# Units 0 and 1 by seven block products in all four block pairs, early narrowing moved, and the last product split over two tiles

## The chip, the core and the metric

The kernel runs on one core of a Trainium2 chip. Such a core has a matrix engine (PE; its weight loads are listed apart as PEld), a vector engine (DVE), a scalar engine (ACT), GpSimd (POOL) and SyncE (SP); here POOL and SP mostly issue DMAs. The engines run their own instruction lists in order and wait for one another through semaphores. The metric is the device time of one execution in microseconds, as the median of several.

## What is computed

An attention block over 32 memory slots gives x (4608 tokens of 512), a soft mixture of experts turns it into x = c @ slot_out with 32 slots, and a two-layer softplus network follows, cut here to what the change touches:

```python
slot_out = ...                         # 32 x 512, from 8 experts (w1, w2)
x = c @ slot_out                       # 4608 x 512, c is a softmax over 32 slots
h = x @ w_in                           # w_in 512 x 2048
g = np.maximum(h, 0.0) + np.log1p(np.exp(-np.abs(h)))
return g @ w_out                       # w_out 2048 x 512
```

## The kernel before

**Stages.** Attention, the softmaxes and the expert layers take the first 178 us. The sum over all experts stands in two PSUM tiles S; when the last product into S is done, S is copied out and multiplied, and the softplus network begins. Its first layer is shortened: x @ w_in = c @ (slot_out @ w_in), so PE forms G = slot_out @ w_in once (`Gs`) and then h for 128 features and 512 tokens with one product of 512 columns (tile `hp`). CT holds c, transposed in nine groups (`stack`, tiles c4 and ctp, L1177 to L1188).

**Units, blocks, jobs.** The 2048 features are eight units of 256, the 4608 tokens nine blocks of 512. ACT takes softplus of h (PSUM to SBUF), and g is then split in a rounded copy (ACT) and the rest (DVE), since one product in PE's format is not exact enough; each product with w_out is three matrix products (rounded x rounded, rounded x rest, rest x rounded). A job is a block, or a pair of blocks, with some units; `JOBS` lists them in order, and PE works through them in this order (`all_out`).

A plain job (`plain_out`, L1587) needs 24 products of 512 columns for each unit and block. A pair job (`seven_out`, L1720) takes two blocks and the two halves of a unit's 256 features and of the 512 outputs as a 2 x 2 block product, by seven block products in place of eight: 42 products for a unit and two blocks instead of 48. For that DVE forms differences of the two blocks' g (`differences`, four instructions of 1024 elements for two units) and of the weights, and seven splits are needed (`split`: ACT L1666, DVE L1668) where a plain job needs four. The block products, named 1 to 7, stand in two PSUM tiles OB (`ob`); each must be read before its tile is used again. `evacuate` reads them: the first step of an output is a copy (ACT or DVE, L801), a second is an addition on DVE (L1368). An output that was written before is added to in HBM by an accumulating DMA from POOL (L1375); a first write goes by SP (L1379).

Before, the jobs are: blocks 0 to 8 plain with units 0 and 1; block 8 plain with 2 and 3, then the four pairs with 2 and 3; block 8 plain with 4 to 7, then the four pairs with 4 to 7 (two groups of two units, products of 24 instead of 12 instructions). So units 2 to 7 are done by seven products, units 0 and 1 are not.

**Narrowing.** w_in and w_out come as 64-bit floats in sixteen pieces wi0, wo0 to wi7, wo7 (w_in and w_out of a unit). `narrow` (L1090 to L1163) makes a piece 32 bits wide with six DVE instructions (L1107, L1111, L1115, L1120, L1127, L1133). For wo it makes the rounded copy (ACT, L1143) and the rest (DVE, L1145), tile W; and for a unit that is used in pair jobs also four quarter-sized sums and differences (L1158), again split in two (ACT L1161, DVE L1163), tile WS.

**What sets the order.** All is written by a planner (`Flow`): it takes of the steps that could begin first the one of lowest rank, and the numbers in `PLAN` shift the ranks. Buffers are pools: four g buffers (`ng`), two h tiles, four output buffers (`ob`), a few x buffers for softplus results, ten weight slots. Weight pieces are loaded by SP in the order `ko`; `ea` says after which expert the first four are put in.

**The end.** The last product (4 of the last job) goes into the two halves t of one OB tile; `finish(..., apart=True)` adds each half on DVE (L1395) and stores it on its own.

Of the kernel before, what the change touches and what calls it, by code (L numbers as in the profile page):

```python
# [26 lines left out]
    "win": 0.1,  # L27
# [28 lines left out]
    "half": 4,  # L56

    "gs": -3667.66,

    "hs": 658.45,  # L60
# [3 lines left out]
    "ea": (1, 5, 5, 5),  # L64
# [3 lines left out]
    "fh": 710.35,  # L68

    "fG": -11197.15,  # L70

    "fo": 12974.77,

    "fe": -3681.57,

    "nb": 2795.97,

    "ns": 2697.86,

    "pace": PACE,  # L80
# [3 lines left out]
    "ob": 4,  # L84

# [18 lines left out]
    "fx": 11238.0,  # L104
# [9 lines left out]
    "ne": 60,  # L114

    "ha": -3.0,

    "va": 3.0,
# [18 lines left out]
class Flow:  # L137
# [9 lines left out]
    def __init__(self):  # L147
        self.engine = defaultdict(float, D=2.1, V=2.2, G=5.7, A=2.0)
        self.token, self.pools, self.got, self.live = {}, {}, {}, []
        self.now = (0.0, "")  # L150
        self.product, self.moved = None, []
# [76 lines left out]
    def run(self, until):  # L228
        stuck = None
        while any(until(c) for c in self.live):  # L230
# [22 lines left out]
            for i, (e, d) in enumerate(ops):  # L253
                t = max(self.seen(now, e), self.engine[e]) + d
# [12 lines left out]
def tile_slot_attention_soft_moe_softplus_mlp(  # L267
# [775 lines left out]

    def load_wo(u):
        yield [("D", 2.52)], [f"+w8<{NW8}"], 0
# [5 lines left out]
        done(f"wo{u}")  # L1051

    def load_wi(u):
        yield [("D", 2.52)], [f"+w8<{NW8}"], 0
# [5 lines left out]
        done(f"wi{u}")  # L1060
# [33 lines left out]
    def narrow(key, after=(), by_act=False, low_by_act=False):  # L1094
# [49 lines left out]
        yield [("V", 1.2)], []  # L1144
        nc.vector.tensor_tensor(out=w[:, 1], in0=af, in1=w.bitcast(F32)[:, 0], op=ALU.subtract)  # L1145
# [7 lines left out]
        for o, x, y, op in (  # L1153
# [3 lines left out]
            yield [("V", 0.37)], []  # L1157
# [4 lines left out]
        yield [("V", 1.23)], []  # L1162
        nc.vector.tensor_tensor(out=w[:, 1], in0=af, in1=w.bitcast(F32)[:, 0], op=ALU.subtract)  # L1163
# [7 lines left out]
    def stack():  # L1171

        for k in range(NTB):
# [14 lines left out]
            nc.scalar.activation(CT[:, 4 * k : 4 * k + 4], ctp, AF.Copy)  # L1188

# [91 lines left out]

    for n, x in enumerate(EARLY + LATE):
        unit = PLAN["pace"][n]
        after = (unit,) if unit else ()
        flow.add(narrow(x, after, n in PLAN["abs"], n in PLAN["rnd"]), PLAN["nb"] + PLAN["ns"] * n, "fb")
    flow.AFTER = {**flow.AFTER, "D": PLAN["land"]}
    flow.run(lambda c: c[2] == "ex")
# [11 lines left out]
    def narrow_G(nb):  # L1299
# [20 lines left out]
        for u in range(2):  # L1320
            for j in (2 * u, 2 * u + 1):
                yield [("D", 0.45)] * 4, []
# [32 lines left out]
    def evacuate(steps, places):  # L1355
# [16 lines left out]
        for half, tb, before, mine in places:  # L1372
            if before:
                yield [("G", 1.0)], before
                nc.gpsimd.dma_start(out=place(half, tb), in_=o, accum_op=ALU.add)  # L1375
                landed(mine, 6.5)
            else:
                yield [("D", 0.8)], []
                nc.sync.dma_start(out=place(half, tb), in_=o)  # L1379
                landed(mine, 4.0)  # L1380
        flow.later("ob", i, 6.5 if before else 4.0)

    def finish(half, tb, before, begin, steps, apart=False):


        yield [("D", 0.8)], [*before, begin, "+ob"], 0
# [3 lines left out]
        landed(f"fin{half}{tb}", 5.0)  # L1390
        for name, at, release in steps:
            for t in range(1 + apart):
                x = slice(t, t + 1) if apart else slice(0, 2)
                yield [("V", 0.69 if apart else 1.22)], [f"{name}{t if apart else 1}", f"fin{half}{tb}"]
# [5 lines left out]
            done(f"rd{name}")  # L1400
        if not apart:
# [17 lines left out]
    JOBS = PLAN["jobs"]  # L1419
# [147 lines left out]
    def plain_out(j, n, tb, units):  # L1567

        for u in units:
            first_u, last_u = u == units[0], u == units[-1]  # L1570
            for (chunks, t0, t1), now, oc in [
# [7 lines left out]
                yield [("P", 0.233 * len(chunks) * len(now))], (  # L1579
# [23 lines left out]
    def raw(j, side, units, m, chain):  # L1603
# [3 lines left out]
        key = j, side, units  # L1607
        yield [("P", 0.467)], [f"G{u}.0", f"G{u}.1", "+h"] + chain[:1]
# [25 lines left out]
    def differences(j, k, units):  # L1634
# [6 lines left out]
        t2 = X[j][:, k, :n]  # L1641
# [3 lines left out]
        yield [("V", d)], [f"t{j}"]  # L1645
        tt(out=t2, in0=b[:, :, 1], in1=a[:, :, 1], op=ALU.subtract)
# [6 lines left out]
        done(f"d{j}{u}4")  # L1653

    def split(j, q, k, units, chain):
# [15 lines left out]
        if q in ("43" if len(groups(JOBS[j][1])) == 1 else "47"):  # L1671
            free("x", Xi[j, side, units])
        if q == "6" and units[-1] == JOBS[j][1][-1]:
            free("x", Xi[j])
# [9 lines left out]
    def groups(units):  # L1684
        return [units[i : i + 2] for i in range(0, len(units), 2)]

    def runs(units):

        n = len(groups(units))
        if n == 1:  # L1690
            return [(q, 0) for q in "1265734"]
        return [("2", 0), ("1", 0), ("2", 1), ("1", 1), ("3", 0), ("3", 1), ("6", 0), ("6", 1)] + [
            ("5", 0), ("7", 0), ("7", 1), ("5", 1), ("4", 0), ("4", 1)
        ]
# [4 lines left out]
    def seven_out(j, units):  # L1699

        for q, k in runs(units):
            grp = groups(units)[k]
# [27 lines left out]
            free("g", i)  # L1730
        over(j, units)
# [162 lines left out]
```

## Time and profile before

| | |
|---|---|
| time, median of three executions | 584.86 us (584.58 to 586.16) |
| the profiled execution's own time | 586.26 us |
| its span, first to last instruction | 584.5 us |
| PE busy | 558.0 us, 95% |
| DVE busy | 403.4 us, 69% |
| ACT busy | 339.0 us, 58% |

The span is cut into 40 slices on the profile's page; a digit gives an engine's busy tenths, and the row PEclk the clock that PE was granted. From 180 us on PE is full; DVE is full only from about 190 to 262 us.

### The profile page before, as it was taken

To read this page: it belongs to the slowest core of one execution; us is meant where nothing else is said; L and a number is where in the kernel's file an instruction comes from. 1 tells how busy PE (TensorE), PEld (TensorE's weight loads), DVE (VectorE), ACT (ScalarE), POOL (GpSimd) and SP (SyncE) were. 2 spreads that over 40 slices of the span, in tenths; PEclk is the share of its full clock that TensorE was granted. 3 is DMA by queue.
4 is the path that set the end of the run, shared out by engine and by line. 5 is a ranking of instruction groups with operands and counts; after the bars stand their busy time and mean duration, and the time that the engine had idled before them with its cause. 6 is when DMAs were issued, how large, how long until landed. Compare 5 with 4: busy or idle time off the path is not lost.

```text
span 584.5 us, 10019 instructions
## 1 busy us (share of the span) xinstructions
PE 558.0 (95%) x4090; PEld 425.5 (73%) x4090; DVE 403.4 (69%) x519; ACT 339.0 (58%) x488; POOL 67.2 (11%) x84
## 2 busy tenths in 40 slices
PE   8798988999879999999999999999999999999997
PEld 4466664545438788878888888888888888888885
DVE  3677855753484999998893877965745945847743
ACT  3667755323324775565866776568567577576530
POOL 1021231300000000000001111210111220211100
PEclk9999998899979999999999999999999999999999
DMA  8999999999999824422215647662255684775952
GB/s 331 424 417 421 417 419 417 418 412 388 418 417 419 344 90 153 151 111 113 86 73 89 107 75 128 108 106 39 46 80 92 101 120 68 115 125 96 178 100 108
DMA packets 23949, 121.56 MB, mean 208 GB/s; under 512 B 3168, under 2 KB 4832, under 8 KB 15712
## 3 DMA queue, kind: packets, MB, share of 16 engines
q1 hardware_dynamic: 17280, 96.81, 41.3%
q0 software_dynamic: 6624, 24.12, 25.9%
q8 instruction: 32, 0.52, 0.4%
q14 instruction: 13, 0.11, 0.1%
HBM read 85.00 MB, written 35.13 MB: 206 GB/s over the span
## 4 chain that ended last, share of the span: by engine, by line
PE 75%; DVE 16%; DMA 3%; ACT 3%; issue 2%; SPq 0%; POOL 0%; DVEq 0%; POOLq 0%; ACTq 0%
PE ob L1720 39%; PE ob L1587 12%; PE hp L1613 4%; DMA kv<-in_kv_dram 3%; PE hid L1203 3%; PE kvp L493 2%; DVE arena L1120 2%; DVE g L1552 2%; PE S L1237 2%; PE idle L920 2%; DVE arena L1133 1%; PE rp L573 1%; PE sc L612 1%; DVE arena L1111 1%; DVE arena L1115 1%
## 5 line engine op out<-in xcount | busy, mean ns | idle before, releaser
L1587 PE MATMUL ob<-g,W 128*128 128x512 f32 x576 | 138.1, 390 | 0.3 <-ACT outs L801 0.3
L1720 PE MATMUL ob<-g,WS 128*128 128x512 f32 x576 | 135.1, 389 | 0.0
L1587 PEld LDWEIGHTS ob<-g,W 128*128 128x128 f32 x576 | 107.7, 188 | 23.8 <-ACT outs L801 1.2
L1720 PEld LDWEIGHTS ob<-g,WS 128*128 128x128 f32 x576 | 108.1, 188 | 22.4
L1720 PE MATMUL ob<-g,W 128*128 128x512 f32 x432 | 100.5, 389 | 0.0
L1668 DVE TENSOR_TENSOR g<-arena,g 128x1024 fp32r<-128x1024 f32 x56 | 67.8, 1222 | 46.6 <-ACT g L1666 46.5
L801 ACT ACTIVATE outs<-ob 128x1024 f32<-128x1024 f32 x61 | 62.5, 1027 | 61.5 <-PE ob L1720 38.6
L1720 PEld LDWEIGHTS ob<-g,W 128*128 128x128 f32 x432 | 81.1, 188 | 16.8
L1375 POOL DMA_DIRECT2D out_dram<-outs x46 | 40.3, 896 | 393.8 <-ACT outs L801 299.5
L1666 ACT ACTIVATE g<-arena 128x1024 fp32r<-128x1024 f32 x56 | 59.2, 1058 | 25.2 <-PE ob L1720 21.1
L1624 ACT ACTIVATE arena<-hp 128x1024 f32<-128x1024 f32 x32 | 32.1, 1021 | 5.7 <-DVE g L1668 3.9
L1552 DVE TENSOR_TENSOR g<-arena,g 128x1024 fp32r<-128x1024 f32 (+1 forms) x26 | 27.3, 1057 | 8.2 <-ACT g L801 6.2
L1668 DVE TENSOR_TENSOR g<-room,g 128x1024 fp32r<-128x1024 f32 x14 | 17.0, 1222 | 20.7 <-ACT g L1666 20.7
L801 ACT ACTIVATE g<-arena 128x1024 fp32r<-128x1024 f32 (+1 forms) x24 | 22.8, 952 | 14.4 <-PE ob L1587 13.6
L1613 PE MATMUL hp<-CT,Gs 128*128 128x512 f32 x96 | 28.9, 389 | 0.0
L920 PE MATMUL idle<-zero 128*128 128x512 bf16 x99 | 27.4, 417 | 1.5 <-POOL zero L923 1.5
L1539 ACT ACTIVATE arena<-hp 128x1024 f32<-128x1024 f32 (+1 forms) x26 | 23.1, 889 | 9.6 <-PE hp L1504 8.8
L666 POOL TENSOR_TENSOR a<-s,ssm 128x512 f32<-128x512 f32 (+1 forms) x20 | 18.8, 961 | 62.9 <-DVE r L465 24.7
L1668 DVE TENSOR_TENSOR g<-x,g 128x1024 fp32r<-128x1024 f32 x14 | 17.0, 1220 | 9.5 <-ACT g L1666 9.5
L1613 PEld LDWEIGHTS hp<-CT,Gs 128*128 128x128 f32 x96 | 18.0, 188 | 3.7
L493 PE MATMUL kvp<-kv,et 128*32 128x128 f32 x512 | 18.6, 275 | 1.7 <-DMA kv<-in_kv_dram 1.7
L920 PEld LDWEIGHTS <-zero 128*128 128x128 bf16 x99 | 9.9, 107 | 13.6 <-issue 5.9
(188 smaller groups left out, 721.5 us busy)
## 6 DMA issues: line engine op xcount, KB each, us to landing
w<-in_moe_w_dram SPq DMA_DIRECT2D x31, 1024.0 KB, 19.9
out_dram<-outs POOLq DMA_DIRECT2D x46, 512.0 KB, 5.4
kv<-in_kv_dram SPq DMA_DIRECT2D x7, 2304.0 KB, 25.0
out_dram<-outs SPq DMA_DIRECT2D x20, 512.0 KB, 2.8
q<-in_q_dram SPq DMA_DIRECT2D x8, 1024.0 KB, 21.7
wi<-in_w_in_dram SPq DMA_DIRECT2D x8, 1024.0 KB, 17.4
wo<-in_w_out_dram SPq DMA_DIRECT2D x8, 1024.0 KB, 17.5
phi<-in_phi_dram SPq DMA_DIRECT2D x8, 576.0 KB, 19.6
```

The source lines that it names most:

```text
L493: nc.tensor.matmul(kvp[32 * h : 32 * h + 32], lhsT=rows[:, 32 * h : 32 * h + 32], rhs=rows_of[:, c, h] if c < SC else rest[:, h], start=(c ...
L801: nc.scalar.activation(o, i, AF.Copy)
L920: nc.tensor.matmul(idle[0], lhsT=zero[:, :128], rhs=zero, start=True, stop=True)
L1375: nc.gpsimd.dma_start(out=place(half, tb), in_=o, accum_op=ALU.add)
L1539: nc.scalar.activation(x, hp, AF.Softplus)
L1552: nc.vector.tensor_tensor(out=g[:, 1, i, t], in0=x, in1=g.bitcast(F32)[:, 0, i, t], op=ALU.subtract)
L1587: nc.tensor.matmul(bank(oc), lhsT=W[u][:, w, i, c], rhs=hb[tb, u][:, x, i], start=(fresh and i == chunks[0] and k == "0"), stop=(stop and ...
L1613: nc.tensor.matmul(hp[:, i], lhsT=Gs[:, 128 * fc : 128 * fc + 128], rhs=CTf[:, TB * tb : TB * tb + TB], start=True, stop=True,)
L1624: nc.scalar.activation(X[key][:, m], hp, AF.Softplus)
L1666: nc.scalar.activation(g[:, 0], x, AF.Copy)
L1668: nc.vector.tensor_tensor(out=g[:, 1], in0=x, in1=g.bitcast(F32)[:, 0], op=ALU.subtract)
L1720: nc.tensor.matmul(OB[at][:, t], lhsT=(W if w == "W" else WS)[u][:, x, c, cols], rhs=g[:, y, m], start=(fresh and u == grp[0] and n == 0), ...
```

## The change

**Jobs.** Units 0 and 1 are now plain in block 8 alone and go through all four pairs as single-group pair jobs. Units 4 and 5, and 6 and 7, get block 8 and three pairs each, and the last pair with all four of these units is the final job. There are 19 jobs: 0 is block 8 with units 0, 1; 1 to 4 are the pairs with them; 5 is block 8 with 2, 3; 6 to 9 the pairs; 10 block 8 with 4, 5; 11 to 13 three pairs; 14 block 8 with 6, 7; 15 to 17 three pairs; 18 the last pair with 4 to 7. In jobs 1, 3, 6 and 9 (`apart`) each block product is read by its own copy and added in HBM; in the others products are still added on DVE.

**Counts from the changed program.** L1587 has 192 products (576 before), L1720 and the new `last_out` 1344 (1008), `hp` 144 as before. DVE has 112 splits L1668 (84), 64 differences (48), 35 whole and three half additions from PSUM (17 and 2), 5 whole and 6 half plain splits L1552 (20 and 8), 32 quarter sums (24). The rest of W and WS is made on DVE ten times (14); for wo3, wo4 and wo7 it is made by ACT (the negative) and an accumulating DMA from POOL (`lower`). POOL issues 66 DMAs (46).

**Order around S.** Of the early pieces, `ea` puts the last three after expert 4 instead of 5, and the ranks now come from a due time for each job less a lead for each kind of step. On DVE, just ahead of the last products into S, this stood before (c are the groups of `stack`, waited for by PE; the L11xx between are the narrowing of wo0 and wi1, in their shared work space arena):

```order
L1179 TENSOR_TENSOR c_2268<-room,c_2268 128x8x32
L1107 TENSOR_SCALAR arena_1948<-wo 128x1024
L1111 TENSOR_SCALAR arena_1948<-arena_1948 128x1024
L1115 TENSOR_SCALAR arena_1948<-arena_1948 128x1024
L1120 SCALAR_TENSOR_TENSOR arena_1948<-wo,arena_1948 128x1024
L1127 TENSOR_SCALAR arena_1948<-wo 128x1024
L1179 TENSOR_TENSOR c_2307<-room,c_2307 128x8x32
```

And now, ahead of the same last two groups:

```order
L1208 TENSOR_TENSOR c_2256<-room,c_2256 128x8x32
L1164 ISA arena_1954<-arena_1954 128x2048 x2
L1208 TENSOR_TENSOR c_2306<-room,c_2306 128x8x32
L1123 TENSOR_TENSOR W<-arena_1954,W 128x1024
L1188 TENSOR_TENSOR arena_1954<-arena_1954 128x256 x2
L1208 TENSOR_TENSOR c_2321<-room,c_2321 128x8x32
L1188 TENSOR_TENSOR arena_1954<-arena_1954 128x256 x2
L1208 TENSOR_TENSOR c_2340<-room,c_2340 128x8x32
```

The narrowing of wo0 and wi1 has moved ahead of groups 5 and 6, and only two and a half instructions stand between the last groups.

**Order of DVE in the first pair job.** In job 1 the splits of units 0 and 1 (L1741), their differences (L1706 to L1716) and the narrowing of later pieces (L1138 to L1164) now share DVE:

```order
L1741 TENSOR_TENSOR g<-room,g 128x1024
L1716 TENSOR_TENSOR room<-room,arena_2521 128x2x512
L1741 TENSOR_TENSOR g<-x_2526,g 128x1024
L1164 ISA arena_2521<-arena_2521,arena_1954 128x2048
L1138 TENSOR_SCALAR arena_2521<-wi 128x1024
L1142 TENSOR_SCALAR arena_2521<-arena_2521 128x1024
L1741 TENSOR_TENSOR g<-x_2526,g 128x1024
```

Before, a plain split L1552 stood between the same narrowing instructions, one for 24 products of PE; now one for 12, and differences with it.

**The end on PE.** The last rows before, block products 5 and 4 (ob_2504 and ob_2503 are the two tiles OB):

```order
L1720 MATMUL ob_2504<-g,WS 128x512 x24
L1720 MATMUL ob_2503<-g,WS 128x512 x12
L1720 MATMUL ob_2504<-g,W 128x512 x24
```

And now:

```order
L1788 MATMUL ob_2524<-g,WS 128x512 x24
L1788 MATMUL ob_2523<-g,WS 128x512 x12
L1816 MATMUL ob_2524<-g,W 128x512 x12
L1816 MATMUL ob_2523<-g,W 128x512 x12
```

Product 4's second half now has the other tile, which product 5 must have left.

```diff
 PLAN = {
-    "ea": (1, 5, 5, 5),
+    "ea": (1, 4, 4, 4),
+    "low": (7, 9, 10, 13, 15),
+    "apart": (1, 3, 6, 9),
     "jobs": (
-        tuple((tb, (0, 1)) for tb in range(9))
-        + ((8, (2, 3)),) + tuple((pair, (2, 3)) for pair in ((0, 1), (2, 3), (4, 5), (6, 7)))
-        + ((8, (4, 5, 6, 7)),) + tuple((pair, (4, 5, 6, 7)) for pair in ((0, 1), (2, 3), (4, 5), (6, 7)))
+        (8, (0, 1)), ((2, 3), (0, 1)), ((6, 7), (0, 1)), ((0, 1), (0, 1)), ((4, 5), (0, 1)),
...
+        (8, (6, 7)), ((4, 5), (6, 7)), ((0, 1), (6, 7)), ((2, 3), (6, 7)), ((6, 7), (4, 5, 6, 7)),
     ),
...
+    def lower(w, af, name, by_dma):
+        if by_dma:
+            yield [("A", 1.06)], []
+            nc.scalar.activation(w[:, 1], af, AF.Copy, scale=-1.0)
+            yield [("G", 1.0), ("D", 3.14)], [], 1
+            nc.gpsimd.dma_start(out=w.bitcast(F32)[:, 1], in_=af, accum_op=ALU.add)
+            landed("l" + name, 2.3)
+            yield [], ["l" + name]
+        else:
+            yield [("V", 1.22)], []
+            nc.vector.tensor_tensor(out=w[:, 1], in0=af, in1=w.bitcast(F32)[:, 0], op=ALU.subtract)
...
         for name, at, release in steps:
-            for t in range(1 + apart):
+            for t, part, b in ((0, 0, at), (1, 0, at), (1, 1, at ^ 1)) if apart else ((0, 1, at),):
                 x = slice(t, t + 1) if apart else slice(0, 2)
-                nc.vector.tensor_tensor(out=o[:, x], in0=OB[at][:, x], in1=o[:, x], op=ALU.add)
-                if apart:
+                nc.vector.tensor_tensor(out=o[:, x], in0=OB[b][:, x], in1=o[:, x], op=ALU.add)
+                if apart and t == part:
...
+    def last_out(j, units):
+        at = bank_of(j, "4")
+        w, c, half = OF["4"]
+        for t in range(2):
+            o = at ^ t
+            for k, grp in enumerate(groups(units)):
...
+                        nc.tensor.matmul(
+                            OB[o][:, t],
+                            lhsT=W[u][:, x, c, cols],
+                            rhs=item[j, "4", grp][0][:, y, m],
+                            start=(t == 1 and k == m == n == 0),
...
-        flow.add(narrow(x, after, n in PLAN["abs"], n in PLAN["rnd"]), PLAN["nb"] + PLAN["ns"] * n, "fb")
+        flow.add(
+            narrow(x, after, n in PLAN["abs"], n in PLAN["low"]),
+            use[u] - LEAD["n" + kind] + PLAN["jit"][n], "fb",
+        )
...
-            flow.add(evacuate(steps, [order(o, where[side])]), PLAN["fe"], "fb")
+            for steps in [[x] for x in steps] if j in PLAN["apart"] else [steps]:
+                flow.add(evacuate(steps, [order(o, where[side])]), due[j, adds[0], 0] + 2.8 - LEAD["e"], "fb")
```

## Rows read from the trace of the kernel before

**Rows 1.** Products of 512 columns: line, count, busy us, mean ns, idle before

```profile
L1587 PE MATMUL ob<-g,W 128*128 128x512 f32 x576 | 138.1, 390 | 0.3 <-ACT outs L801 0.3
L1720 PE MATMUL ob<-g,WS 128*128 128x512 f32 x576 | 135.1, 389 | 0.0
L1720 PE MATMUL ob<-g,W 128*128 128x512 f32 x432 | 100.5, 389 | 0.0
```

**Rows 2.** Busy us by stretch: PE, PEld, DVE, ACT, POOL, clock, DMA share, GB/s

```profile
160.50:164.30 3.80, 0.03 (x1) 0.00 (x0) 3.69 (x6) 1.85 (x3) 0.00 (x0) 1.00 1.00 416
166.00:172.00 6.00, 5.52 (x54) 2.17 (x46) 5.66 (x7) 0.77 (x2) 0.00 (x0) 0.50 1.00 412
...
190.00:262.00 72.00, 71.97 (x371) 58.64 (x369) 70.03 (x90) 45.66 (x55) 0.00 (x0) 1.00 0.47 172
...
310.00:390.00 80.00, 80.00 (x354) 66.25 (x353) 61.28 (x54) 51.80 (x53) 13.02 (x15) 1.00 0.64 102
```

**Rows 3.** The chain that ended last, its last stretch of PE: start, us, what

```profile
516.23 63.93 PE ob L1720 x282
```

**Rows 4.** Around S, by start: PE's last groups and experts, SP's last load

```profile
164.31 0.66 PE L1185 MATMUL ctp<-ident,c 128*128 128x128 f32 x4 [3.77 <-DVE c L1179]
164.89 2.91 PE L1203 MATMUL hid<-w,room 128*32 128x256 f32 x32
...
175.69 2.80 PE L1237 MATMUL S<-w,hT 128*32 128x256 f32 x48
...
181.67 0.50 PE L1504 MATMUL hp<-CT,Gs 128*128 128x512 f32 x1
...
157.22 2.77 SPq L1038 DMA_DIRECT2D w<-in_moe_w_dram  x2
```

**Rows 5.** The same last load (L1038, the two halves of the last w2), issue to landing

```profile
DMA to landing us min/median/max: 17.5/18.1/18.7
```

**Rows 6.** DVE by start: differences, additions and splits, narrowing and quarter sums

```profile
295.97 1.23 DVE L1643 TENSOR_TENSOR room<-x,room 128x1024 f32<-128x1024 f32 x1
297.23 1.23 DVE L1646 TENSOR_TENSOR arena<-x,room 128x1024 f32<-128x1024 f32 x1
298.37 1.22 DVE L1649 TENSOR_TENSOR x<-x 128x1024 f32<-128x1024 f32 x1
...
316.77 1.22 DVE L1368 TENSOR_TENSOR outs<-ob,outs 128x1024 f32<-128x1024 f32 x1
317.90 1.21 DVE L1668 TENSOR_TENSOR g<-x,g 128x1024 fp32r<-128x1024 f32 x1
...
221.18 1.80 DVE L1158 TENSOR_TENSOR arena<-arena 128x256 f32<-128x256 f32 x4
222.90 0.69 DVE L1107 TENSOR_SCALAR arena<-wi 128x1024 int32<-128x1024 int32 x1
...
226.95 1.22 DVE L1552 TENSOR_TENSOR g<-arena,g 128x1024 fp32r<-128x1024 f32 x1
228.08 1.22 DVE L1133 CUSTOM_DVE_ANT_0 arena<-arena 128x2048 uint16<-128x2048 uint16 x1
229.22 0.69 DVE L1107 TENSOR_SCALAR arena<-wi 128x1024 int32<-128x1024 int32 x1
```

**Rows 7.** The end, by start: DVE's last two additions

```profile
580.18 1.29 DVE L1395 TENSOR_TENSOR outs<-ob,outs 128x512 f32<-128x512 f32 x2 [3.08 <-PE ob L1720]
```

**Rows 8.** POOL's first accumulating DMA, a later one, and DVE's two casts

```profile
308.69 1.02 POOL L1375 DMA_DIRECT2D out_dram<-outs  x1 [183.20 <-ACT outs L801]
...
386.95 0.87 POOL L1375 DMA_DIRECT2D out_dram<-outs  x1 [7.30 <-DVE outs L1368]
...
386.46 0.68 DVE L803 CAST g<-x 128x1024 fp32r<-128x1024 f32 x1
```

**Rows 9.** L1127 by piece, first and last start; L1375, issue to landing

```profile
L1127 DVE TENSOR_SCALAR arena<-wo x8: 693/694/695, 157.7 to 284.8; 128x1024 int32<-128x1024 uint32 x8
...
DMA to landing us min/median/max: 5.1/5.3/6.5
```

More of the change, by code (lines that the diff above doesn't have):

```diff
@@ L25 @@
 PLAN = {
-    "win": 0.1,
+    "win": 0.05,
     "split": 7,
@@ L150, in __init__ @@
         self.now = (0.0, "")
-        self.product, self.moved = None, []
+        self.product, self.moved, self.stretch = None, [], {}
     def keep_warm(self, t):
@@ L1059, in load_wi @@
         raw_t["wi", u], at["wi", u] = t, flow.got["w8"]
-        done(f"wi{u}")
+        arrived("wi", u)
+    hold = {x: (token,) for x, token in PLAN["hold"]}
     def weight_loads():
@@ L1188, in stack, with groups, runs @@
             nc.scalar.activation(CT[:, 4 * k : 4 * k + 4], ctp, AF.Copy)
+    def groups(units):
+        return [units[i : i + 2] for i in range(0, len(units), 2)]
+    def runs(units):
+        n = len(groups(units))
+        if n == 1:
+            return [(q, 0) for q in "1265734"]
+        return [("2", 0), ("1", 0), ("2", 1), ("1", 1), ("3", 0), ("3", 1), ("6", 0), ("6", 1)] + [
+            ("5", 0), ("7", 0), ("7", 1), ("5", 1), ("4", 0), ("4", 1)
+        ]
     nc.scalar.preload_act_table_set("softplus")
@@ L1280, in tile_slot_attention_soft_moe_softplus_mlp @@
     flow.add(stack(), -15000.0, "ex")
+    JOBS = PLAN["jobs"]
+    LEAD = PLAN["lead"]
+    use, due, t = {}, {}, 183.0
+    for j, (where, units) in enumerate(JOBS):
+        for u in units:
+            use.setdefault(u, t)
+        if isinstance(where, int):
+            for u in units:
+                due[j, u] = t
+                t += 5.9
+        else:
+            t += 0.94 * len(units)
+            for q, k in runs(units):
+                due[j, q, k] = t
+                t += 1.36 * len(groups(units)[k])
     for n, x in enumerate(EARLY + LATE):
         unit = PLAN["pace"][n]
-        after = (unit,) if unit else ()
-        flow.add(narrow(x, after, n in PLAN["abs"], n in PLAN["rnd"]), PLAN["nb"] + PLAN["ns"] * n, "fb")
+        after = (unit,) if unit else ("hp0.0",) if n >= len(EARLY) else ()
+        kind, u = x[0], x[1]
+        flow.add(
+            narrow(x, after, n in PLAN["abs"], n in PLAN["low"]),
+            use[u] - LEAD["n" + kind] + PLAN["jit"][n], "fb",
+        )
     flow.AFTER = {**flow.AFTER, "D": PLAN["land"]}
+    for e in "PVA":
+        flow.engine[e] += PLAN["late"]
     flow.run(lambda c: c[2] == "ex")
@@ L1400, in finish @@
             done(f"rd{name}")
+            done(f"rd{name}{half}{tb}")
         if not apart:
@@ L1607, in raw @@
         key = j, side, units
+        fresh = m == 0 and not (side and shared(j, units))
         yield [("P", 0.467)], [f"G{u}.0", f"G{u}.1", "+h"] + chain[:1]
@@ L1682, in tile_slot_attention_soft_moe_softplus_mlp, with shared @@
     ONE = {"1": ("12", 0, 0), "6": ("63", 0, 1), "5": ("57", 1, 1), "4": ("4", 1, 0)}
[L1684 to L1694, printed above, removed]
+    def shared(j, units):
+        return len(units) == 1 and len(groups(JOBS[j][1])) > 1
     def bank_of(j, q):
@@ L1701, in seven_out @@
         for q, k in runs(units):
+            if q == "4" and j == len(JOBS) - 1 and len(groups(units)) == 2:
+                if k:
+                    yield from last_out(j, units)
+                continue
             grp = groups(units)[k]
@@ L1789, in tile_slot_attention_soft_moe_softplus_mlp @@
             for half in range(2):
-                flow.add(evacuate([(f"s{j}.{half}", half, True)], [order(half, where)]), PLAN["fe"], "fb")
+                flow.add(evacuate([(f"s{j}.{half}", half, True)], [order(half, where)]), due[j, units[-1]] + 5.9 - LEAD["e"], "fb")
             continue
         seen_pair = True
-        r = PLAN["fx"] + 60.0 * j
         gr = groups(units)
+        r = due[j, runs(units)[0][0], 0] - LEAD["x"]
         plan = [(0, g, m) for g in gr for m in range(len(g))]
```

143 lines of the change are left out of this document (91 added, 52 removed).

## The prediction

> **What bounds the kernel now.** I read the busy times by stretch first. In 310 to 390 us PE is busy 80.00 of 80.00 us and DVE 61.28 [rows 2]: PE sets the pace. In 190 to 262 us DVE is nearly as full, 70.03 of 72, and yet PE loses only 0.03 [rows 2]: DVE at 97% did not starve PE there. Then the groups of products: from 182 us to the end PE waited 0.3 us in total ahead of the products that fill `ob` [rows 1]. The chain that ended last ends in 282 products of 512 columns in 63.93 us, 0.2267 us each [rows 3]; the 390 ns that the groups show is the length of one with its overlap [rows 1], not its price. So from 182 us on time goes down where products are taken away, as long as DVE keeps up. Before 178 us the bound is another: the last load into the expert layer (below).
>
> The sums are made on the span, 584.5 us, of an execution of 586.26; the median of the three runs, 584.86, is 0.36 above the span, and I keep that distance. About 0.3% is what a measurement can tell from no change.
>
> **The products.** Units 0 and 1 in eight blocks cost 2 x 8 x 24 = 384 products; by seven block products they cost 2 x 4 x 42 = 336. The groups say the same: 576 + 576 + 432 = 1584 before [rows 1], 192 + 1344 = 1536 now; the products into `hp` stay 144. So 48 x 0.2267 = **10.9 us** less, all on the path as long as PE is full.
>
> **S.** The narrowing that stood ahead of the last two groups of c made PE wait 3.77 us, and then expert 6 started at 164.89 [rows 4]. That seems to promise as much. But the last w2 comes in two halves, issued at 157.22 and, as the pair of issues ends at 157.22 + 2.77 and one takes 0.33, at 159.66 [rows 4]. They landed 17.5 and 18.7 us after issue [rows 5]. The pairing 157.22 + 18.7 and 159.66 + 17.5 gives 175.9 and 177.2; the other gives 178.4 for the second, which can't be: the last 48 products end at 175.69 + 2.80 = 178.49 [rows 4], and the eight of the second half, 0.47 us at that pace, began at 178.0. So S can end at 177.2 + 0.47 = 177.7 at the earliest, 0.8 us sooner, as long as the DMA engines, full in that stretch (share 1.00) [rows 2], bring the same bytes in the same time; the four early pieces are loaded ahead of it in both orders. Against it, ACT now makes WS of unit 1 ahead of the last hT, which could cost 1.5 us more, about one and a half such steps. I take **0.4 less**, from 0.8 less to 1.5 more.
>
> **The end.** After PE's last product DVE now does two half additions in 1.29 us, 0.69 one alone [rows 7], though the first half's products had ended earlier: both read a tile that PE still writes. With product 4 in two tiles the first half is added while PE does the second, 12 x 0.2267 = 2.7 us, and one addition is left: **0.6 less**. In the same 2.7 us DVE must make two additions of product 5's tile, 2 x 1.13; that just fits, and if not, the gain is gone: 0 to 0.6.
>
> **What DVE must do instead.** This is the price. An addition or split, 1.22 us long, costs 1.13 from start to start when the next doesn't depend on it; a difference 1.26 or 1.14, say 1.20; the five first instructions of narrowing 226.95 - 222.90 = 4.05 and the sixth 1.14, a piece 5.19; four quarter sums 1.72 [rows 6]. Counted in the changed order from the copy of S to the 71st block product, the first of job 13, by when all narrowing is done: 70 splits, 17 additions, 6 rests of W or WS and 3 plain splits, 96 x 1.13 = 108.5; 40 differences, 48; 12 pieces, 62.3; 24 quarter sums, 10.3; 15 short ones at no more than half a microsecond, 7. That is 236 us. PE has up to there 3.2 us from the end of S to its first `hp` [rows 4] and 1090 products of 512 columns, 247.1: 250 us. So DVE is asked for 94%, less than the 97% of 190 to 262. Copies that are moved to ACT need no sum: ACT had 45.66 of 72 us even there [rows 2]. After job 13 DVE has 16 us of work for each job of 92 products, 20.9 us, about as in 310 to 390.
>
> Evenly spread that would cost nothing. It isn't: taken from one job's first product to the next one's, DVE's sum is above PE's at three places, by 1.1 us (job 3 to 4), 2.5 (6 to 7) and 6.8 (11 to 12: nine at 1.13, four differences, two pieces less one instruction, four quarter sums, 26.7 against 88 x 0.2267 = 19.9). DVE must have run ahead. With four g buffers a split can be ready three block products ahead, 3 x 12 x 0.2267 = 8.2, less the split itself, 1.2 on DVE and about as much on ACT: 5.8. That covers the first two places and leaves 1.0 at the third. To both sides: nothing at all is lost if the pattern of 190 to 262 holds [rows 2]; 1.1 + 2.5 + 6.8 = 10.4 if DVE is never ahead. I take **2.5 more**, near the low end, for the 1.0 and some waits between DVE, ACT and PE that a sum doesn't see: 12 products now hang on a split where there were 24, and DVE's additions wait for PE in the same queue.
>
> The three rests by POOL are off DVE; their DMA lands in about 5.3 us [rows 9] and is hidden if the piece was ready that early, else it is among the 10.4. SP's stores stand behind the loads of wi6, wo5 and others that wait for a slot; what is behind them is a store, and with four output buffers that costs nothing until four stand.
>
> **Sum.** 584.5 - 10.9 - 0.4 - 0.6 + 2.5 = 575.1, and 0.36 on top: **575.5**. With every term at its better end 584.5 - 10.9 - 0.8 - 0.6 = 572.2, with all at the worse 584.5 - 10.9 + 1.5 + 10.4 = 585.5, both as spans.
>
> **Rivals.** *DVE takes over as the bound (slower).* If the mixed order costs more than 1.13 a piece, because splits wait for ACT's copy or additions for PE, DVE sets the pace to job 13 from 250 / 236 = 6% on; each further 1% is 2.4 us, and at 11% the 11.9 us gained are gone. At 13% it is 236 x 1.13 = 267, 17 us more: 584.5 - 11.9 + 17 = 589.6. PE would also lose its clock: after it idled for 3.8 us the granted clock fell to 0.50, the 1.2 GHz level [rows 2], and expert 6's and 7's products took 2.91 us and more [rows 4]. For it: narrow margins in four jobs in a row. Against: 97% was carried [rows 2].
>
> *POOL's DMAs beside narrowing.* The first accumulating DMA stood at 308.69 [rows 8], the last narrowing of its kind at 284.8 [rows 9]: they never met. Now jobs 6 and 9 add every block product in HBM while pieces are narrowed. Four output buffers at seven reads in 20.9 us must come back within 11.9 us. Product 2 waits for product 1's landing: read at 3.0, issued at 6.3, landed at 11.6, held 8.6. If an issue is late by d, 2d is added, and reads stall from d = 1.65 on. Were POOL held off for three narrowing instructions, 3 x 0.72 = 2.2, each such pair (1 and 2, 5 and 7) would be 1.1 late, 4.4 in the two jobs, and W or WS by POOL might come late as often: 4.4 to 8, so 580 to 583. Against: beside a cast one issue took 0.87 [rows 8], though a landing near there took 6.5 and not 5.3 [rows 9]. The Trainium skill, page "SBUF — State Buffer", section "SBUF: two separate sides", has a rule for it: a DMA from GpSimd has its descriptors written by GpSimd, and GpSimd is shut out of the port it shares with VectorE while VectorE runs an instruction in a two-port mode, a `tensor_scalar` or copy between SBUF tensors. By that rule this rival comes true as often as the two meet; no run here shows it yet.
>
> *S is not held by the load.* Then the 3.4 us from 178.49 to about 175.1 come too: 572.1.
>
> **Chances.** Forecast, 572 to 579: 0.60. POOL: 0.13 (0.11 of it still faster by over 0.3%, 0.02 same). S earlier: 0.07. DVE as the bound: 0.20 (0.03 faster, 0.07 same, 0.10 slower). So faster 0.81, same 0.09, slower 0.10. The range goes from 571 to 584: it takes in the forecast, S earlier, POOL and the mild part of the DVE case, and leaves out its heavy part and a better end than I see.
>
> **What would show it.** Right: 1536 products in L1587's and L1720's places at 0.2267; PE full from 182 us on but for some 2.5 us, most of it around the start of job 12; the last products of S starting within a microsecond of 178; one addition after the last product. Wrong: PE waiting for DVE's splits job after job between 200 and 430 us, or a granted clock below 1 there; ACT's reads waiting for `out_dram` DMAs, with POOL's landings well over 5.3; S done at 175.

## The result, and the profile after

| | before | after |
|---|---|---|
| median | 585.49 us (584.58 to 587.14, 5 runs) | 576.00 us (575.89 to 576.16, 5 runs) |
| span of the profiled execution | 584.5 us | 573.9 us |
| first `hp` to the end of PE's last product | 398.49 us [rows 3, 4] | 389.74 us |

The ratio of the medians is 0.983, 95% interval 0.980 to 0.986: 1.7% faster, well over the 0.3% that can be told from no change. The forecast was 575.5.

The page of after, its first part (busy time, share of the span, instructions):

```profile
PE 545.9 (95%) x4048; PEld 415.5 (72%) x4048; DVE 450.7 (79%) x567; ACT 373.9 (65%) x525; POOL 86.7 (15%) x104
```

PE's products by line, which answer to [rows 1]: count, busy us, mean ns, idle before:

```profile
L1788 PE MATMUL ob<-g,WS 128*128 128x512 f32 x768 | 181.7, 389 | 0.0
L1788 PE MATMUL ob<-g,W 128*128 128x512 f32 x552 | 129.9, 390 | 1.5 <-ACT outs L813 1.5
L1648 PE MATMUL ob<-g,W 128*128 128x512 f32 x192 | 47.1, 391 | 0.2 <-ACT outs L813 0.2
L1816 PE MATMUL ob<-g,W 128*128 128x512 f32 x24 | 5.6, 390 | 0.0
```

They are 1536 products as counted, and from 178 us on PE never waited for DVE. What it did wait for is ACT's reading of an output tile, 1.7 us where it was 0.3. Two of the stretches of [rows 2] again (busy us of PE, PEld, DVE, ACT, POOL, clock, DMA share, GB/s):

```profile
190.00:262.00 72.00, 70.89 (x340) 58.10 (x339) 68.35 (x68) 57.78 (x62) 5.69 (x6) 1.00 0.58 172
310.00:390.00 80.00, 80.00 (x381) 65.97 (x380) 74.72 (x78) 65.55 (x71) 19.57 (x21) 1.00 0.83 144
```

DVE is now nearly as full from 310 to 390 us, 74.72 where it was 61.28, and PE still loses nothing there. The 1.11 us that PE lost from 190 to 262 us is a single gap. PE and ACT around it, by start:

```profile
196.31 0.84 PE L1648 MATMUL ob<-g,W 128*128 128x512 f32 x3
198.26 0.96 PE L1788 MATMUL ob<-g,W 128*128 128x512 f32 x3 [1.11 <-ACT outs L813]
...
194.99 1.02 ACT L813 ACTIVATE outs<-ob 128x1024 f32<-128x1024 f32 x1
197.19 1.02 ACT L813 ACTIVATE outs<-ob 128x1024 f32<-128x1024 f32 x1 [1.19 <-PE ob L1648]
```

Job 0, plain, fills its second output tile last; ACT begins to read it when PE's product ends, at 197.19. Job 1's first block product goes into the same tile, so PE stands until 198.26, though the other tile had been read by 196.01. The same meeting of a plain job and a pair job comes at the starts of jobs 5, 11 and 15 (282.06, 395.26 and 471.94 us). Taken from start to start against 0.2266 us a product, which holds in both traces wherever PE is full, these four borders cost 1.41, 0.52, 0.55 and 0.53 us, **3.0** in all; before, the two places where PE lost time cost 0.94. That is 2.07 more, and 398.49 - 48 x 0.2266 + 2.07 = 389.7: the stretch is explained to 0.1 us.

S and the end, by start:

```profile
174.21 1.83 PE L1278 MATMUL S<-w,hT 128*32 128x256 f32 x24 [0.70 <-DMA w<-in_moe_w_dram]
176.65 0.64 PE L1278 MATMUL S<-w,hT 128*32 128x256 f32 x8 [0.61 <-DMA w<-in_moe_w_dram]
180.47 0.49 PE L1565 MATMUL hp<-CT,Gs 128*128 128x512 f32 x1
...
564.58 5.63 PE L1816 MATMUL ob<-g,W 128*128 128x512 f32 x24
570.24 0.69 DVE L1456 TENSOR_TENSOR outs<-ob,outs 128x512 f32<-128x512 f32 x1 [1.46 <-PE ob L1816]
```

PE's last products into S wait for the load itself, the eight of the last half from 176.65 on; `hp` begins 1.2 us earlier than in [rows 4]. The second half of the last w2 was issued at 159.66 before and at 159.13 now, and in both it landed as long after its issue:

```profile
DMA to landing us min/median/max: 17.5/17.5/17.5
```

So it was there at 177.2 before and at 176.6 now. The eight products that need it began 0.7 us later than that before, and at once now. Before:

```profile
177.87 0.61 PE L1237 MATMUL S<-w,hT 128*32 128x256 f32 x8
```

At the end one half addition stands after PE's last product where two did [rows 7].

### The profile page after: what moved, and what is told of

It is laid out like the page before. It is cut to its first block, busy times and chain, and to the rows that moved or that the text cites. A ratio compares the mean times of both kernels' runs of the same rounds, so it can differ in the third digit from the quotient of the medians.

```text
span 573.9 us, 10098 instructions
## 1 busy us (share of the span) xinstructions
PE 545.9 (95%) x4048; PEld 415.5 (72%) x4048; DVE 450.7 (79%) x567; ACT 373.9 (65%) x525; POOL 86.7 (15%) x104
## 4 chain that ended last, share of the span: by engine, by line
PE 77%; DMA 13%; DVE 6%; ACT 3%; issue 1%; POOL 0%; DVEq 0%; POOLq 0%; SPq 0%
PE ob L1788 52%; DMA w<-in_moe_w_dram 8%; PE ob L1648 7%; PE hp L1675 5%; DMA kv<-in_kv_dram 5%; PE idle L932 3%; PE kvp L505 2%; DVE ssm L661 1%; PE ob L1816 1%; DVE s L631 1%; PE tp L688 1%; DVE smx L629 1%; ACT outs L813 1%; PE hp L1565 1%; PE rp L585 1%
## 5 line engine op out<-in xcount | busy, mean ns | idle before, releaser
L1788 PE MATMUL ob<-g,WS 128*128 128x512 f32 x768 | 181.7, 389 | 0.0
L1788 PEld LDWEIGHTS ob<-g,WS 128*128 128x128 f32 x768 | 144.0, 188 | 30.2 <-issue 0.4
L1788 PE MATMUL ob<-g,W 128*128 128x512 f32 x552 | 129.9, 390 | 1.5 <-ACT outs L813 1.5
L1788 PEld LDWEIGHTS ob<-g,W 128*128 128x128 f32 x552 | 103.3, 188 | 24.3 <-ACT outs L813 2.8
L813 ACT ACTIVATE outs<-ob 128x1024 f32<-128x1024 f32 x78 | 80.1, 1027 | 57.9 <-PE ob L1788 47.8
L1741 DVE TENSOR_TENSOR g<-arena,g 128x1024 fp32r<-128x1024 f32 x55 | 66.8, 1221 | 22.8 <-ACT g L1739 22.6
L1648 PE MATMUL ob<-g,W 128*128 128x512 f32 x192 | 47.1, 391 | 0.2 <-ACT outs L813 0.2
L1430 DVE TENSOR_TENSOR outs<-ob,outs 128x1024 f32<-128x1024 f32 x30 | 36.7, 1222 | 8.0 <-PE ob L1788 7.8
L1648 PEld LDWEIGHTS ob<-g,W 128*128 128x128 f32 x192 | 35.9, 188 | 8.0 <-ACT outs L813 0.6
L1741 DVE TENSOR_TENSOR g<-x,g 128x1024 fp32r<-128x1024 f32 x28 | 33.9, 1221 | 7.5 <-ACT g L1739 7.3
L1741 DVE TENSOR_TENSOR g<-room,g 128x1024 fp32r<-128x1024 f32 x29 | 35.1, 1220 | 2.9 <-ACT g L1739 2.8
L1739 ACT ACTIVATE g<-room 128x1024 fp32r<-128x1024 f32 x29 | 30.6, 1058 | 5.9 <-PE ob L1788 4.7
L1739 ACT ACTIVATE g<-x 128x1024 fp32r<-128x1024 f32 x28 | 29.6, 1057 | 4.0 <-PE ob L1788 4.0
L1278 PE MATMUL S<-w,hT 128*32 128x256 f32 x256 | 17.4, 407 | 4.8 <-ACT hT L1264 3.4
```

What stands on the lines that cost most here:

```text
L813: nc.scalar.activation(o, i, AF.Copy)
L1430: nc.vector.tensor_tensor(out=o, in0=OB[at], in1=o, op=ALU.add)
L1648: nc.tensor.matmul(bank(oc), lhsT=W[u][:, w, i, c], rhs=hb[tb, u][:, x, i], start=(fresh and i == chunks[0] and k == "0"), stop=(stop and ...
L1739: nc.scalar.activation(g[:, 0], x, AF.Copy)
L1741: nc.vector.tensor_tensor(out=g[:, 1], in0=x, in1=g.bitcast(F32)[:, 0], op=ALU.subtract)
L1788: nc.tensor.matmul(OB[at][:, t], lhsT=(W if w == "W" else WS)[u][:, x, c, cols], rhs=g[:, y, m], start=(fresh and u == grp[0] and n == 0), ...
```

## The experiments

Times are medians; each group was timed beside the kernel before, and e5 is the changed kernel once more. The most exact measure is the stretch from the first `hp` to the end of PE's last product: in after, e2, e5, e7 and e12, whose products are in the same order, it is 389.74, 389.66, 389.72, 389.71 and 389.74 us.

### The border tile: e1, e6, with e5 beside them

```
-        return int(q in "235") ^ (len(JOBS[j][1]) == 4 or j % 2)
+        return int(q in "235") ^ BASE[j] ^ (len(JOBS[j][1]) == 4)
+    BASE, end = [], 1
+    for where, units in JOBS:
+        BASE.append(1 - end)
+        end = 1 - BASE[-1] if isinstance(where, int) else BASE[-1]
```

(and plain jobs begin with tile BASE[j]).

> The changed kernel, but where a plain job and a pair job meet, the next job's first product goes into the PSUM tile that was left first, not into the one that PE has just filled (at the starts of jobs 1, 5, 11 and 15; all else by the same rules). In the changed kernel's trace PE starts these four jobs 1.41, 0.52, 0.55 and 0.53 us later than one product after another would, 3.0 us in total, while ACT reads the tile just filled (1.03 us). Theory (the hand-over of the tile is all that PE still waits for after 182 us): the four waits go, 576.0 - 3.0 = 573.0, and PE's product groups show no idle time. Rival (DVE, asked for 94%, is what PE really waits for, and the border only hides it): PE waits for DVE's splits instead, 1.5 us or more of it, and the time stays at 574.5 to 576.

> The changed kernel itself, once more beside the next three, so that they are compared on the same chip: 575.5 to 577; first hp to the end of the last product 389.7 us as before, with the same four waits at the starts of jobs 1, 5, 11 and 15.

> The kernel of e1 once more, beside the changed kernel: in e1 the stretch from the first hp to the end of the last product was 387.36 us instead of 389.74. Theory: that repeats to 0.1, since no other stretch is touched, and the median is 2.4 us below that of the changed kernel on this chip. Rival (what is gained is lost in the stages ahead of S or in the run to run spread): medians within 1 us of one another.

Measured: e1 575.11 (572.92 to 575.49: two runs near 573, three near 575.3), ratio to before 0.980 [0.977, 0.984]; by its median alone it would fall into the rival's range. On one chip e5 took 576.14 (575.86 to 576.53), ratio 0.983 [0.980, 0.987], and e6 573.28 (572.60 to 573.91), ratio 0.978 [0.975, 0.981]. The stretch was 387.36 in both e1 and e6, so 2.4 us shorter, of 3.0 expected. All that PE waits for in e6 after 178 us (us, times, longest):

```profile
PE ob L1792 <- DVE g L1745: 0.4, 1, 0.4
```

The four waits are gone, so the theory holds, and 0.7 comes back at one place, in job 4, where PE waits 0.38 us for a split and the products around it lose another 0.3. The row names DVE, but the split had itself stood as long for ACT's copy:

```profile
264.36 1.22 DVE L1745 TENSOR_TENSOR g<-room,g 128x1024 fp32r<-128x1024 f32 x1 [0.38 <-ACT g L1743]
```

So here too it is not DVE's load that PE meets. This kernel is faster than both, by 2.9 us than the changed one on the same chip. What made three runs of e1 2 us longer no row shows.

### Room on DVE: e7, e8

```
         nc.vector.tensor_tensor(out=g[:, 1], in0=x, in1=g.bitcast(F32)[:, 0], op=ALU.subtract)
+        nc.vector.tensor_tensor(out=dump, in0=dump, in1=dump, op=ALU.mult)
```

> The changed kernel with one more DVE instruction behind each of the 112 splits, a product of a 128x128 tile of its own that nobody reads (about 0.25 us, between the 0.29 of a difference of 64x128 alone and the 0.43 of a quarter sum of 128x256 in a row); the order of everything else stays. Up to job 13 that is 70 x 0.25 = 17 us on DVE, which is busy 240.0 of 259.6 us there in the changed kernel. Theory (DVE has the 14 to 20 us of room that the sum said, PE's lead of 3 to 4 us evens out the rest): 0 to 5 us more, 576 to 581, PE's waits now for DVE's splits. Rival (DVE is already the bound job by job, with under 1 us of room in a job of 21): 10 to 17 us more, 586 to 593.

> As e7, with a 128x256 tile: about 0.43 us behind each split, 70 x 0.43 = 30 us up to job 13. Theory (room of 14 to 20 us, after which DVE sets the pace, each further microsecond on DVE being one of the time): 10 to 16 us more than the changed kernel, 586 to 592, and about 12 more than e7. Rival (already the bound): 25 to 30 us more, 601 to 606. Behind job 13 DVE has 16 + 7 x 0.43 = 19 us of work in a job of 20.9, so nothing is lost there.

Measured: e7 575.52 (574.58 to 577.19), e8 581.96 (581.11 to 583.23); stretches 389.71 and 396.11. DVE in e7, three instructions in a row, by start:

```profile
301.13 0.28 DVE L1744 TENSOR_TENSOR dump<-dump 128x128 f32<-128x128 f32 x1
301.33 1.22 DVE L1743 TENSOR_TENSOR g<-room,g 128x1024 fp32r<-128x1024 f32 x1
302.47 0.28 DVE L1744 TENSOR_TENSOR dump<-dump 128x128 f32<-128x128 f32 x1
```

The two stretches again in e7 (PE, PEld, DVE, ACT, POOL, clock, DMA share, GB/s):

```profile
190.00:262.00 72.00, 70.89 (x339) 58.09 (x338) 71.43 (x90) 58.15 (x62) 5.41 (x6) 1.00 0.58 170
310.00:390.00 80.00, 80.00 (x394) 65.83 (x387) 78.96 (x102) 65.62 (x71) 18.98 (x22) 1.00 0.84 147
```

And the second of them in e8:

```profile
310.00:390.00 80.00, 78.14 (x393) 62.45 (x392) 79.45 (x100) 62.51 (x69) 18.81 (x22) 1.00 0.80 135
```

One instruction more costs 0.20 us from start to start (301.33 - 301.13), so e7 put 70 x 0.20 = 14.0 us on DVE up to job 13. DVE then is busy 71.43 of 72 us and PE loses no more than before: the same 70.89, the same stretch to 0.03. In e8 it is 0.34 each (305.22 to 305.56 in its trace), 23.8 us where 30 were written, and 6.4 us are lost where 10 to 16 were. The longest of PE's waits that name DVE are there for additions, which leave an output tile late:

```profile
PE ob L1791 <- DVE outs L1430: 1.5, 3, 0.8
```

So the room ends between 14 and 23.8 us; if each further microsecond costs one, at 17.4. That is the theory's size (14 to 20); both rivals, which had DVE as the bound already, fall.

### The same room used for real work: e9, e10, e11

```
-    "low": (7, 9, 10, 13, 15),
+    "low": (),
```

is e9; `"apart": ()` for `(1, 3, 6, 9)` is e10; both together are e11.

> The changed kernel with the rests of wo3, wo4 and wo7 made on DVE as for the others, not by ACT and an accumulating DMA from POOL: six more DVE instructions, 6 x 1.13 = 6.8 us up to job 13. Theory (e7 and e8: room for 14 to 17 us on DVE up to job 13): the time stays, 575.5 to 577. Rival (the rests come at a place where DVE has no room, as where its sum stands 6.8 us above PE's ahead of job 12): PE waits there, 2 to 6 us more, 578 to 582.

> The changed kernel with the products of jobs 1, 3, 6 and 9 added on DVE as in the other jobs, not each copied and added in HBM: 12 more additions on DVE, 12 x 1.13 = 13.6 us, 12 copies fewer on ACT and 12 accumulating DMAs fewer on POOL. Theory (room of 14 to 17 us, but an addition can hold DVE until PE has ended the product): 0 to 3 us more, 576 to 579. Rival (as additions wait for PE in DVE's queue, the splits behind them come late in each of the four jobs): 4 to 8 us more, 580 to 584.

> Both of e9 and e10: 20.4 us more on DVE up to job 13 than in the changed kernel. Theory (room of 14 to 17.4 us, then one for one): 3 to 6.4 us more, 579 to 582.5. Rival (the room is in places that this order can't use, or the planner moves work to where it has room): under 1 us or over 8 us more.

Measured beside a before of 586.49: e9 576.71 (575.85 to 577.40), ratio 0.983 [0.980, 0.986], as after. But **e10 597.32** (596.60 to 598.81), ratio 1.019 [1.016, 1.022], and e11 593.14 (590.69 to 594.14), ratio 1.011 [1.008, 1.014]: both slower than the kernel before. The stretches are 391.01, 411.02 and 408.19. For e9 the theory holds; its stretch is 1.3 us longer, and PE still waits for ACT alone. For e10 both numbers written were too small. For e11 the rival's "over 8 us more" came true. What PE waited for in e10 (us, times, longest):

```profile
PE ob L1648 <- DMA W<-arena: 6.7, 1, 6.7
PE ob L1788 <- DVE g L1741: 4.6, 2, 2.3
PE ob L1788 <- ACT outs L813: 3.4, 3, 1.2
PE hp L1675 <- ACT arena L1688: 1.3, 1, 1.3
```

How an addition does that shows in e10's trace near 266 us, DVE and PE by start:

```profile
266.38 1.23 DVE L1430 TENSOR_TENSOR outs<-ob,outs 128x1024 f32<-128x1024 f32 x1 [0.73 <-PE ob L1788]
267.52 1.21 DVE L1741 TENSOR_TENSOR g<-room,g 128x1024 fp32r<-128x1024 f32 x1
268.79 1.83 PE L1788 MATMUL ob<-g,WS 128*128 128x512 f32 x5 [2.29 <-DVE g L1741]
```

DVE at the same place in e5, the changed kernel:

```profile
264.46 1.22 DVE L1741 TENSOR_TENSOR g<-room,g 128x1024 fp32r<-128x1024 f32 x1
265.60 1.22 DVE L1741 TENSOR_TENSOR g<-arena,g 128x1024 fp32r<-128x1024 f32 x1
267.56 1.23 DVE L1430 TENSOR_TENSOR outs<-ob,outs 128x1024 f32<-128x1024 f32 x1 [0.74 <-PE ob L1788]
```

Both additions wait 0.7 us for PE. In e5 two splits stand ahead of it, and PE has work; in e10 the split that PE needs next stands behind it, so DVE waits for PE and then PE for DVE. The same comes once more, at 382.48. The second kind of loss is narrowing that came late: the rest of W of wo3 was issued by POOL only at 290.54, 21 us later than in after, and landed 10.0 us later still, beside three loads of weights. The issue in after, and PE's next products in e10, by start:

```profile
269.59 0.87 POOL L1118 DMA_DIRECT2D W<-arena  x1 [8.33 <-ACT W L1116]
...
300.57 2.50 PE L1648 MATMUL ob<-g,W 128*128 128x512 f32 x5 [6.68 <-DMA W<-arena]
```

And e10's busy times, clock and DMA share in the stretches of the wait and behind it (the columns as above):

```profile
291.00:300.50 9.50, 2.89 (x13) 2.06 (x11) 8.33 (x8) 3.15 (x4) 0.56 (x1) 0.81 0.95 284
300.50:303.10 2.60, 2.53 (x6) 2.05 (x7) 2.41 (x6) 0.71 (x1) 0.00 (x0) 0.50 0.01 5
```

The clock that PE was granted fell from 0.81 in the stretch of the wait to 0.50 behind it, and five products took 2.50 us instead of 1.30 (four steps of 0.2266 and 0.39 for the last). From start to start, slow products included, the two places behind an addition cost 4.2 and 4.1 us and the wait for W 8.4: 16.7 of the 21.3 us by which the stretch grew.

e11, where DVE makes that rest itself, has no such DMA wait and is 4.2 us faster than e10 with 6.8 us more on DVE. It has the two places behind an addition (4.0 and 4.2 us), and its largest loss, 9.3 us from 463 to 476, is where PE waits for ACT. DVE, ACT and PE there, by start:

```profile
459.42 1.23 DVE L1430 TENSOR_TENSOR outs<-ob,outs 128x1024 f32<-128x1024 f32 x1 [0.74 <-PE ob L1788]
461.01 1.06 ACT L1191 ACTIVATE WS<-arena 128x1024 fp32r<-128x1024 f32 x1 [4.75 <-DVE arena L1188]
465.98 2.13 PE L1675 MATMUL hp<-CT,Gs 128*128 128x512 f32 x4 [2.21 <-ACT x L1688]
```

ACT had stood 4.75 us for quarter sums; the last two of the four stood in DVE's queue behind a split and two additions, the second of which waited for PE. From 461 us on ACT had no gap until 473, and PE waited for it three times. It is the same cause once removed, as these rows read; no run tests this place alone.

### S: e3, e4

```
-    "ea": (1, 4, 4, 4),
+    "ea": (1, 4, 4, 7),
```

is e3, and `(1, 5, 5, 5)` is e4.

> The changed kernel, but the last early piece, wo1, is loaded after the last w2 instead of ahead of it (1 MB, 2.5 us at the 410 GB/s of that stretch). Theory (S ends by the landing of the last w2): the last products of S start 2.5 us earlier, at 174.1 instead of 176.65, and PE's first hp at 178.0 instead of 180.47, unless ACT's hT then ends last (it made PE wait 3.4 us there), in which case 1 to 2 us earlier. What comes of it at the end depends on wo1, narrowed later: from 2 us less (574) to none. Rival (S is held by the chain of ACT and PE through hs, hTp and hT): the last products of S start within 0.5 us of 176.65.

> The changed kernel with the last three early pieces loaded after expert 5 again instead of 4, as before the change; the four pieces are still ahead of the last w2, but land some 5 us later, and DVE narrows them after the last groups of c. Theory (S ends by the landing of the last w2, and the narrowing has slack until 185 us): S's last products start within 0.6 us of 176.65; the time is 576.0 to 577.5, the rest being narrowing that runs later into jobs 0 and 1. Rival (the earlier pieces are what brought S forward by 1.2 us): S's last products start at 178 again and the time is 577 to 578.

Measured: e3 578.53 (578.20 to 582.31), ratio 0.989 [0.986, 0.992]; e4 579.02 (577.87 to 582.35), ratio 0.989 [0.985, 0.992]. PE in e3, by start:

```profile
171.82 2.80 PE L1278 MATMUL S<-w,hT 128*32 128x256 f32 x48
174.69 1.19 PE L1302 MATMUL sop<-sel,s2s 128*128 128x128 f32 x8
180.77 0.80 PE L1565 MATMUL hp<-CT,Gs 128*128 128x512 f32 x1 [2.77 <-DVE Gs L1513]
```

With one piece less ahead of it the last half landed at 173.7, 2.9 us earlier than in after, S's last 48 products run without a wait, and `sop` starts at 174.69, 2.5 us earlier than in after (177.22): S follows the load. More than that is lost again, and the time lies above what was written for this run: wo1 is then narrowed just where DVE should make the difference for `Gs`, PE waits 2.77 us for it, and the stretch behind is 392.29 us, 2.55 longer than in after. Part of that is the clock (the columns as above):

```profile
181.00:184.00 3.00, 3.00 (x12) 2.71 (x13) 2.76 (x5) 1.77 (x4) 0.00 (x0) 0.50 1.01 421
```

In after it is 1.00 in these 3 us. What PE waited for in e4 from 160 to 178 us:

```profile
PE ctp L1214 <- DVE c L1208: 3.7, 1, 3.7
PE S L1278 <- DMA w<-in_moe_w_dram: 1.4, 2, 0.7
```

In e4 the wait of [rows 4] for a group of c is back, 3.7 us, and S's last eight products still began at 176.27, held by the load. So that wait costs S nothing. The time was more than either range written: DVE's copy of S came 1.5 us late, behind quarter sums of the pieces that had landed later, and `hp` began at 182.83. In the changed order the earlier pieces are thus worth near 3 us of time, not by S but by what DVE would still have to do right behind it.

### The end: e2

```
-            o = at ^ t
+            o = at
```

and `finish` adds both halves from that tile.

> The changed kernel with block product 4 of the last job in the two halves of one tile again, as before the change; all else as changed. Theory (both half additions read a tile that PE still writes, so none begins until PE ends): two half additions, 1.29 us, stand after PE's last product instead of one of 0.69, so 0.6 us more, 576.6. Rival (the half additions were bound by their own products, not by the tile): one addition remains after PE's end, 576.0.

Measured: 576.78 (576.09 to 578.03), ratio 0.984 [0.981, 0.987]. PE's last product ended at 571.00 and DVE's two half additions after it:

```profile
571.04 1.29 DVE L1456 TENSOR_TENSOR outs<-ob,outs 128x512 f32<-128x512 f32 x2 [3.08 <-PE ob L1816]
```

1.33 us to DVE's end instead of 0.72, with the same stretch ahead of it: 0.6, as the theory says. The medians agree, but could not show it alone.

### POOL beside DVE's tensor_scalar: e12

```
+        nc.vector.tensor_scalar(out=dump, in0=dump, scalar1=1.0, scalar2=None, op0=ALU.mult)
```

> As e7, but the instruction behind each split is a tensor_scalar of 128x256 in SBUF, the kind of narrowing's first steps, not a tensor_tensor; about 0.2 us each, 22 us in all, 14 up to job 13. In the changed kernel's trace 6 of 66 accumulating DMAs issued by POOL took 1.18 to 1.65 us and not 0.87, each with such an instruction in its later part. Theory (POOL is held while DVE runs a tensor_scalar in SBUF, and these DMAs have slack): the median issue grows from 0.87 to 1.0 or more, landings stay near 5.3, and the time stays, 575.5 to 577. Rival (POOL's issues are lengthened by something else): the median stays at 0.87. Rival (POOL's DMAs are what the output buffers wait for): the time grows by more than 1.5 us, with PE or ACT waiting for out_dram.

Measured: 575.16 (574.62 to 576.97), ratio 0.981 [0.978, 0.984], stretch 389.74. The median issue was 0.884 us, where it is 0.872 in after, so that number was missed; but of the issues that don't follow directly on another 20 took 1.01 us or more, against 4 in after and 2 in e7, whose instruction is as long and of the other kind. One of the 20, in e12, POOL and DVE by start:

```profile
333.82 1.01 POOL L1437 DMA_DIRECT2D out_dram<-outs  x1 [7.37 <-DVE outs L1430]
334.47 0.28 DVE L1744 TENSOR_SCALAR dump<-dump 128x256 f32<-128x256 f32 x1
```

One of the long ones in after:

```profile
346.91 1.42 POOL L1437 DMA_DIRECT2D out_dram<-outs  x1 [5.20 <-DVE outs L1430]
347.55 0.69 DVE L1146 TENSOR_SCALAR arena<-arena 128x1024 int32<-128x1024 int32 x1
```

Each of these two issues ends 0.08 to 0.09 us after the `tensor_scalar` beside its last part does (334.83 against 334.75, 348.33 against 348.24). The DMAs landed after 5.6 us in the median (5.3 in after, 5.6 in e5), and no read of an output tile waited for them. So POOL is held, as the theory says, and it costs nothing.

## Why the prediction was right, step by step

**The products: right.** 48 fewer at 0.2266, 10.9 us, and all of it in the stretch once the borders are counted.

**S: the mechanism right, the size mixed with chance.** The forecast was 0.4 less, by the load and not by the 3.77 us wait; e3 and e4 show both halves of that. The last half landed at 177.2 before, as the prediction had worked out, and against that landing S gained 0.64: its last eight products began 0.68 us after it before, and 0.04 to 0.05 after it in all eleven traces whose order up to S is the same (after, e1, e2, e5 to e12). That is within the bound of 0.8. The rest of the 1.2 us between the two traces is that the load itself landed 0.6 earlier. In the eleven traces it landed between 175.6 and 177.8, and the one of before lies among them, so that part is chance. By it the sign "within a microsecond of 178" was missed too, by 0.35.

**The end: right.** 0.6, by e2 and by the two rows.

**The waits: the term's size was right and its cause wrong.** The sum had 2.5 us for DVE, mostly around job 12. DVE cost nothing at all: no wait of PE names it, job 12 lost none, and 14 us more on DVE (e7) still cost none. What failed is the step that set DVE's sum against PE's from job to job, with the lead of four g buffers as all the cover: narrowing needs no g buffer, and is done further ahead than splits. Job 11 in after, from its first product to job 12's (PE, PEld, DVE, ACT, POOL, clock, DMA share, GB/s):

```profile
395.26:415.36 20.10, 20.10 (x89) 16.63 (x90) 16.94 (x18) 14.62 (x16) 4.36 (x5) 1.00 0.68 125
```

DVE had 16.94 us of work there, not the 26.7 of the sum (whose terms as listed make 26.5 at most): nine of the eleven narrowing instructions counted there, the last eleven of all, were done by 395 us. In its place stood 2.07 us that no term had, the four borders. They could have been read from the code: a plain job begins in tile 0 and ends in tile 1, a pair job begins and ends in tile `j % 2`, and the new list puts an odd pair job behind a plain one three times (1, 11, 15) and a plain one behind an even pair job once (5); e1 and e6 take them away. With measured terms 584.5 - 10.9 - 1.2 - 0.6 + 2.1 = 573.9, the span of after; of the 1.2, half is the chance of the load.

**From span to median: wrong, and made up by luck.** The 0.36 us was taken as a distance that stays. But every execution lasts longer than its own span, by 1.7 to 1.8 us before and by 2.1 in after. It came out as 0.36 because the profiled execution of before was itself 1.4 us slower than the median. So the distance was 1.7 too small and the forecast's span 1.2 too long; that the forecast came within 0.5 us is in part luck.

**The rival "DVE takes over".** It did not come, and its point was well placed for work that waits for nothing: 6% forecast, 14 us carried by e7, 17.4 by e8's slope, which is 7% of 236. For additions it was too mild: in e10 13.6 us, 5.8% by the same count, cost 21 us and made the kernel slower than before, because they stand in DVE's queue until PE is done and put off narrowing. In this planner's order the change is faster only with those additions taken off DVE.

**The rival "POOL's DMAs beside narrowing".** The page "SBUF — State Buffer" of the Trainium skill, section "SBUF: two separate sides", has GpSimd's descriptors held off while VectorE runs in a two-port mode; the traces agree (issues that end 0.09 us after the `tensor_scalar`), though no row shows the mode. The price was not there: five of 66 issues were held, by 0.3 to 0.6 us, and a sixth stood behind one of them, with slack behind them; even 20 long ones (e12) left the stretch at 389.74. The issue that was held against this rival [rows 8] had a cast beside its first 0.2 us only. In after a `tensor_scalar` beside the first half of an issue cost nothing either (0.87 us at 369.47), so that row could not tell.

**The rival "S is not held by the load"** falls by e4, and by PE's wait for the load in after.

## What to carry to other kernels

A busy sum tells how much more an engine can carry only for work that waits for nothing; an instruction that waits for the bounding engine costs its place in the queue, so ask what stands behind it. Where two kinds of phases share a pair of accumulators, check at each border that the next phase begins with the one that was left first. A wait of 3.8 us ahead of a stage that a load ends is worth nothing, while the same load moved ahead by one piece brings that stage forward by 2.5; what DVE then has to do behind it decides whether any of it is kept.

## What the runs showed of the hardware

- DVE was busy 71.43 of 72 us while PE lost nothing but the 1.11 us of a border (e7). An instruction that depends on nothing adds less than its length: 0.20 us where the row says 0.28 (128x128).
- The issue of an accumulating DMA by POOL took 0.87 us, or 1.15 right behind another. With a DVE `tensor_scalar` beside its last part it ended 0.08 to 0.09 us after that instruction (five issues in after; most, but not all, in e12).
- After 6.68 us without work PE's granted clock was 0.50, the 1.2 GHz level, and five products took 2.50 us.
- Eleven executions whose order is the same up to S reached the first `hp` up to 2.3 us apart (179.4 to 181.7), always 3.9 us behind the landing of the last load into S; the 390 us behind it repeated to 0.1 in the five whose products are in the same order.
- An execution lasts longer than its span from first to last instruction by an amount that hardly changes for one kernel: 1.7 to 1.8 us before, 2.1 in after.
